# Eight batches of attention and MoE on one core: fixed attention tiles, a new order of steps, and joined tails

## The chip, the cores and the metric

The kernel runs on one core of a Trainium2 chip. The metric is the device time in microseconds. The program is one launch; nothing is computed on the host.

## What is computed

For each of 8 batches with 8 heads, 576 positions and a head width of 64, two attentions are added: one over q, k and v that are averaged in groups of four positions (144 positions, its result repeated four times), and a local one over the keys that lie at a distance under four. The sum, as a matrix x of 576 rows and 512 columns, goes through a mixing layer:

```python
s = scale * np.matmul(q, k.transpose(0, 1, 3, 2))
mask = np.abs(pos[:, None] - pos[None, :]) < factor      # local part
x = out_up + out_local                                   # (B, S, H * D)
theta = x @ w_theta
zr, zi = x * np.cos(theta), x * np.sin(theta)
y = np.einsum('ts,bsd->btd', w_tok_r, zr) + np.einsum('ts,bsd->btd', w_tok_i, zi)
u = x + y
return u + np.maximum(u @ w_ch, 0.0)
```

Inputs and output are float32; the kernel computes in bfloat16 with float32 sums.

## The kernel before

All eight batches run through one program that is pipelined over the batches by hand. Each kind of work is a Python generator, and a long string, `ORDER` (lines 80 to 88), says which generator takes its next step. After each step `pin` (line 695) chains every new instruction to the one before it on the same engine, so that every engine works in exactly the order of the string. The letters, with steps per batch:

- L (8) and v (5) load q, k and v; C (8) and w (5) cast them to bfloat16 on GpSimd (batch 0's q on ScalarE).
- A (4, `turns`, line 309) turns q and k so that the head width lies on the partitions: A.0 and A.2 are q, A.1 and A.3 are k. For most batches TensorE transposes nine blocks into PSUM; for the batches in `DMA_QK` a DMA transpose does it (q, `turn_qk`, line 284) into an SBUF tile of the staging pool. In both cases ScalarE copies the result in two halves into `qT` or `kT` (line 328), undoing a row order, and VectorE sums groups of four (line 336).
- B (1) averages v; Q (2) and N (3) are the scores and the result of the averaged attention; S (5, line 409) are the local scores: TensorE, then the exponential on ScalarE (line 432), then two selects on GpSimd that cut the band (lines 439 and 441; batch 0 has a mask from TensorE).
- V (5, `outputs`, line 487) is the local result: TensorE into PSUM, VectorE divides into `tmp` (line 508). `tmp` comes from a pool with four buffers; for the batches in `DMA_X` GpSimd first zeroes the rows that the division doesn't write (line 507).
- T (5, line 525) turns `tmp` and adds the averaged part into `xT` (line 542): TensorE and VectorE for most batches, a DMA transpose (t, line 293) and GpSimd for those in `DMA_X`.
- H (5, `phases`) is theta with cosine and sine on ScalarE (lines 564, 565; H.4 is the tail of 64 positions, with a DMA transpose, z). Z (4, `modulate`, line 592) turns x back, on TensorE (line 601) or, for the batches in `DMA_Z`, by one DMA transpose (x, line 301), and multiplies.
- X (5, `mix`, line 612) is the mixing over positions: X.0 to X.3 are 9 matmuls each over 512 columns (line 620), X.4 is 36 over the tail's 64 columns (line 626); VectorE adds x (lines 621, 628) into `uT`.
- u (2, line 631) turns `uT` by two DMA transposes, main part and tail. R (5, `channels`, line 643) multiplies by w_ch, R.4 for the tail with eight matmuls of 64 rows and 256 columns (line 658). O (5, `store`, line 665) adds on VectorE into `osb`, which has four buffers, and issues the stores; the tail has two.
- K, l, c, h, g, W are constants and weights: c.7 to c.11 are the casts of the second token weight on VectorE (line 241), W (9) its transposes. D (5) are warm-up matmuls.

All DMAs are issued by SyncE's queue, SP, in the order of the string. PSUM has two tiles of two banks (w2, taken in turn) and four of one bank (w1, taken in turn).

ScalarE's exponential and sine need different tables, so each change between S or Q and H loads one.

Of the kernel before, what the change touches and what calls it, by code (L numbers as in the profile page):

```python
# [10 lines left out]
BF16 = mybir.dt.bfloat16  # L11
AF = mybir.ActivationFunctionType
ALU = mybir.AluOpType
AX = mybir.AxisListType

P = 128
B = 8
H = 8
S = 576
D = 64  # L20
DM = 512
# [11 lines left out]
NCH = 5  # L33

WR = 9
# [6 lines left out]
HALF = 64  # L42
MAIN = 512
# [4 lines left out]
def kernel(  # L48
# [11 lines left out]
    nc = tc.nc  # L60

    const = ctx.enter_context(tc.tile_pool(name="const", bufs=1))
# [13 lines left out]
    def w1(name, dt=FP32):  # L76
# [1 line left out]


    ORDER = (  # L80
        "KLLLLCCLLKKKLCALCvCvvCCCDvvLLwLLAALLAlvlllSSLwLSwwwVBCCCCQQVNNlllAVcNvvvCTTAcvcTllCCSSHHVVDTTlllALHc"
        "chCccZLLLwwwAwwHHSSDZLzZDcBcSZDcWcLLLCvCCCcQVWWWvQWVCvvWCNWCCwSWWNVwwwXAAhXAvhNAhwLLXTSSLXQQTTLLBuVH"
        "VTggLCCLCgLLHvvgTCCCCCNNHHVHXSSRROzOZZZvLvLAwLLLLZARvvvvvACNSOXwwwASRuCCCSwVXVVOXQCCQCTSVTTTALABLSXA"
        "uTCvSRSwvHNNwHHCOVwwVZXwANLVCLHHRRLLLLQQLLCCCRROOOzOBVTLuSTCCLZLZSTSHNZNHVCXTTAAXvvvvLLAAHHCCwVCCCqw"
        "wLwHvwXzLLVZSXqZZLLCCCQqSuXvVNBROSQZTLTwXVVXNqvTvTTNAvLALASHHHVHwVuXvvHzXZCCwCCAwwSCSRNROXLqQSLqOZRC"
        "BCCqSOVTRTqQRvvuSSOOTZHZVVXTNTNAAHHXVVAHvwwwHtAtwXSSXXRRRRuuOOONOVtVzwTBZZSZRQQRVTSROROOOSSRttZNHNOu"
        "XTVTTNSRxOXHVVHHVtttZZHzXZZVXXXXTttTTuTTXHHRHxROOROuROZHZHRZzZOXXuXXXXuRuRROOOXRRRuOORRROOOORO"
    )

    staged = {}  # L90
# [98 lines left out]
    for i in range(2):  # L189
        t = const.tile([P, NCH, H, 66], BF16, name=f"v_w{i}")  # L190
        nc.vector.memset(t[:, :, :, 64:65], 1.0)
        v_ws.append(t)

    vds = []
    for i in range(2):
        t = const.tile([P, 2, H, 66], BF16, name=f"vd{i}")
# [82 lines left out]
    parts, turned = {}, {}  # L279


    DMA_QK, DMA_X, DMA_Z = (6, 7), (6, 7), (6, 7)

    def turn_qk(b):

# [23 lines left out]
    def turns(b):  # L309

        q_tm, k_tm = inputs.pop(b)
        qT = work.tile([P, 4, S], BF16, tag="qT", name=f"qT{b}")
        kT = kTs[b % 2]
        qdT = work.tile([P, 4, SD], BF16, tag="qdT", name=f"qdT{b}")
        kdP = kdPs[b % 2]
        parts[b] = (qT, kT, qdT, kdP)

        for j in range(4):
            n, i = j % 2, j // 2
            tm, To = ((q_tm, qT), (k_tm, kT))[n]  # L320
            if b in DMA_QK:
                ps = turned.pop((b, j)).rearrange("p r w -> p (r w)")
            else:
                ps = w2(f"pstr{n}{i}_{b}", BF16).rearrange("p k e -> p (k e)")[:, 0:WR * P]
                for r in range(WR):
                    nc.tensor.transpose(out=ps[:, P * r:P * r + P], in_=tm[:, i, r, :, :], identity=ident)  # L326
            for a in range(2):
                act(  # L328
                    out=To[:, 2 * i + a, 0:S].rearrange("p (w r) -> p w r", r=WR),
                    in_=ps.rearrange("p (r a w) -> p a w r", r=WR, a=2)[:, a],  # L330
                )
            hs = slice(2 * i, 2 * i + 2)
            dst, src = (qdT[:, hs, :], qT[:, hs, :]) if n == 0 else (kdP[:, hs, :, 0:30], kT[:, hs, :])
            src = src.rearrange("p e (m j) -> p e m j", j=4) if n == 0 else src.rearrange("p e (g m j) -> p e g m j", g=5, j=4)
            with nc.allow_low_precision(reason="sums are taken in float32 and rounded once"):
                nc.vector.tensor_reduce(out=dst, in_=src, axis=AX.X, op=ALU.add)  # L336
            yield
# [149 lines left out]
    def outputs(b):  # L487

        v_w = v_ws[b % 2]
        for c in range(NCH):  # L490
            kw, qn, cnt = KW[c], QN[c], QC[c]
            ps = w2(f"psloc{c}_{b}")
            pv = ps[:, :, 0:260].rearrange("p e (j w) -> p e j w", w=65)
            for h in range(H):
                blk, par = slot(h)
                nc.tensor.matmul(  # L496
                    out=pv[0:qn, h // 4, h % 4, :],
                    lhsT=pms[b][c][0:kw, 4 * par + blk, 0:qn],
                    rhs=v_w[0:kw, c, h, 0:65],
                    start=(h % 4 == 0), stop=(h % 4 == 3),  # L500
                )
            rl = work.tile([P, 2, 4], FP32, tag="rl", name=f"rl{c}_{b}")
            nc.vector.reciprocal(out=rl[0:cnt], in_=pv[0:cnt, :, :, 64])
            tmp = tmps[b, c] = work.tile([P, DM], BF16, tag="tmp", bufs=4, name=f"tmp{c}_{b}")
            if b in DMA_X:
                lo = 96 if c < 4 else 64
                nc.gpsimd.memset(tmp[lo:], 0.0)  # L507
            nc.vector.tensor_tensor(  # L508
                out=tmp[0:cnt].rearrange("p (e j d) -> p e j d", e=2, j=4),
                in0=pv[0:cnt, :, :, 0:D],  # L510
                in1=rl[0:cnt].unsqueeze(3).to_broadcast([cnt, 2, 4, D]),
                op=ALU.mult,
            )
            yield
        pms.pop(b)


    def parted(t):

        return (t[:, 0:4 * MAIN].rearrange("p (e t) -> p e t", e=4),  # L520
                t[:, 4 * MAIN:4 * S].rearrange("p (e t) -> p e t", e=4))
# [85 lines left out]
            yield  # L607


    uTs, urs = {}, {}  # L610

    def mix(b):

        (xA, xB), z = parted(xTs[b]), zs.pop(b)
        uT = uTs[b] = moep.tile([P, 4 * S], BF16, tag="uT", name=f"uT{b}")
        uA, uB = parted(uT)
        for dc in range(4):
            ps = w1(f"psu{dc}_{b}")
            for j in range(9):
                nc.tensor.matmul(out=ps, lhsT=z[:, j, P * dc:P * dc + P], rhs=WT[:, j, 0:MAIN], start=(j == 0), stop=(j == 8))  # L620
            nc.vector.tensor_tensor(out=uA[:, dc, :], in0=ps, in1=xA[:, dc, :], op=ALU.add)  # L621
            yield
        ps = w1(f"psut_{b}")[:, 0:4 * HALF].rearrange("p (e t) -> p e t", e=4)
        for dc in range(4):
            for j in range(9):
                nc.tensor.matmul(out=ps[:, dc, :], lhsT=z[:, j, P * dc:P * dc + P], rhs=WT[:, j, MAIN:S],  # L626
                                 start=(j == 0), stop=(j == 8))
        nc.vector.tensor_tensor(out=uB, in0=ps, in1=xB, op=ALU.add)
        yield

    def u_turn(b):

        ur = moep.tile([P, 16, P], BF16, tag="ur", name=f"ur{b}")
        utr = moep.tile([P, 2, P], BF16, tag="utr", name=f"utr{b}")
        urs[b] = ur, utr
        nc.sync.dma_start_transpose(out=ur, in_=uTs[b][:, 0:4 * MAIN])
        yield
        nc.sync.dma_start_transpose(out=utr, in_=uTs[b][:, 4 * MAIN:4 * S])
        yield

    rels = {}

    def channels(b):

        uA, uB = parted(uTs[b])
        for c in range(5):
            psr = rels[b, c] = w1(f"psr{c}_{b}")
            if c < 4:
                for dc in range(4):
                    nc.tensor.matmul(  # L650
                        out=psr, lhsT=uA[:, dc, P * c:P * c + P], rhs=wch[:, dc, :],
                        start=(dc == 0), stop=(dc == 3),
                    )
            else:

                for dc in range(4):
                    for hf in range(2):
                        nc.tensor.matmul(
                            out=psr[64 * hf:64 * hf + 64, 0:256], lhsT=uB[:, dc, :],
                            rhs=wch[:, dc, :].rearrange("p (j e d) -> p e j d", j=2, e=2)[:, hf],  # L660
                            start=(dc == 0), stop=(dc == 3),
                        )
            yield

    def store(b):

        ur, utr = urs.pop(b)
        for c in range(5):
            psr = rels.pop((b, c))
            osb = moep.tile([P, DM], FP32, tag="osb", bufs=4, name=f"osb{c}_{b}")  # L670
            n = 4 if c < 4 else 2
            nc.vector.scalar_tensor_tensor(  # L672
                out=osb[:, 0:P * n].rearrange("p (e d) -> p e d", d=P),
                in0=psr[:, 0:P * n].rearrange("p (e d) -> p e d", d=P), scalar=0.0,
                in1=ur[:, c:16:4, :] if c < 4 else utr, op0=ALU.max, op1=ALU.add,
            )
            if c < 4:
                nc.sync.dma_start(out=out[b, P * c:P * c + P, :], in_=osb)
            else:
                for hf in range(2):  # L680
                    nc.sync.dma_start(
                        out=out[b, 512:576, :].rearrange("t (j e d) -> e t j d", j=2, e=2)[hf],
                        in_=osb[64 * hf:64 * hf + 64, 0:2 * P].rearrange("p (j d) -> p j d", j=2),
                    )
            yield

    last = {}
# [57 lines left out]
```

## Time and profile before

| | us |
|---|---|
| median of 8 runs | 252.41 |
| lowest and highest | 250.55, 254.09 |
| the profiled execution's own time | 254.09 |
| its span in the profile | 252.4 |

The profile is of one execution. A row of the groups gives line, engine, operation, what is written and read with partitions x elements, then the busy time and the mean of one in ns, then the idle time just ahead of them and who ended it. A wait's row gives the total, the number of times and the longest. Matmuls overlap, so the busy time of TensorE (PE) is not its work at full speed. The granted TensorE clock is 0.985 in the mean.

### The profile page before, as it was taken

The page shows a single profiled execution, that of the slowest core. Times are in us where ns is not written, and L with a number is a line of the kernel's source. Part 1 is how long each engine was busy: PE and PEld are TensorE (multiplying, and loading weights), DVE is VectorE, ACT ScalarE, POOL GpSimd, SP SyncE. Part 2 cuts the span into 40 slices and gives each one's busy share as a digit, 9 for nine tenths or more (in the row PEclk, how much of TensorE's full clock was granted, in tenths as well). Part 3 has the DMA queues.
Part 4 walks back from the last instruction along what each step waited for, and adds up shares of the span by engine and source line. Part 5 has one row for each costly group of instructions (what it writes and reads, how often), then busy time and mean ns, then how long its engine had stood idle before and what let it go on. Part 6 is the DMA issues. An engine that isn't in the chain of part 4 may idle for free.

```text
span 252.4 us, 6628 instructions
## 1 busy us (share of the span) xinstructions
PE 225.8 (89%) x2602; PEld 136.1 (54%) x2602; DVE 185.5 (74%) x340; ACT 170.1 (67%) x250; POOL 166.9 (66%) x233
## 2 busy tenths in 40 slices
PE   0877799799999999999999999999769989999991
PEld 0535365466577566755657656565445645455450
DVE  3275788758979988898898898899676558365462
ACT  3595799438899559999688999899936781151000
POOL 4438764994898999899679666998199971600000
PEclk9999999779999999999999999999999999999999
DMA  6999989996496999899999999979691765965596
GB/s 209 291 298 359 289 236 350 240 236 229 42 293 171 321 157 246 187 298 223 297 235 271 210 204 225 262 108 216 128 270 35 229 96 101 137 202 117 65 269 198
DMA packets 100511, 53.94 MB, mean 214 GB/s; under 512 B 83968, under 2 KB 86016, under 8 KB 100480
## 3 DMA queue, kind: packets, MB, share of 16 engines
q1 hardware_dynamic: 100480, 53.53, 90.1%
q8 instruction: 20, 0.33, 0.6%
q14 instruction: 11, 0.09, 0.2%
HBM read 33.59 MB, written 9.44 MB: 170 GB/s over the span
## 4 chain that ended last, share of the span: by engine, by line
PE 60%; ACT 11%; DMA 9%; DVE 8%; POOL 8%; issue 2%; SPq 1%; DVEq 0%; POOLq 0%; ACTq 0%
PE psu L620 20%; PE psr L650 7%; PE psth L559 6%; PE pstr L326 4%; PE psloc L496 4%; DMA z<-zT 3%; PE psS L424 3%; ACT pm L432 3%; POOL pm L441 3%; POOL pm L439 2%; ACT qT L328 2%; PE psut L626 2%; DMA out_dram<-osb 2%; PE xTps L538 2%; DMA st_q<-in_q_dram 2%
## 5 line engine op out<-in xcount | busy, mean ns | idle before, releaser
L620 PE MATMUL psu<-WT,z 128*128 128x512 bf16 x288 | 66.8, 379 | 0.6 <-DMA z<-zT 0.6
L439 POOL TENSOR_SCALAR_AFFINE_SELECT pm<-pm 128x1024 bf16<-128x1024 bf16 (+1 forms) x35 | 36.7, 1048 | 21.7 <-ACT pm L432 21.7
L620 PEld LDWEIGHTS <-z 128*128 128x128 bf16 x288 | 26.5, 98 | 29.7 <-DMA z<-zT 1.1
L432 ACT ACTIVATE pm<-psS 128x1024 bf16<-128x1024 f32 (+1 forms) x40 | 37.9, 980 | 5.4 <-PE psS L424 5.0
L441 POOL TENSOR_SCALAR_AFFINE_SELECT pm<-pm 128x1024 bf16<-128x1024 bf16 (+1 forms) x35 | 36.6, 1046 | 2.4
L508 DVE TENSOR_TENSOR tmp<-psloc,rl 120x512 bf16<-120x512 f32 (+2 forms) x40 | 27.6, 690 | 7.6 <-POOL tmp L507 6.0
L650 PE MATMUL psr<-wch,uT 128*128 128x512 bf16 x128 | 30.8, 380 | 1.4 <-DVE uT L621 1.4
L564 ACT ACTIVATE cs<-psth,pihc 128x512 bf16<-128x512 f32 x32 | 22.3, 697 | 14.1 <-PE psth L559 11.4
L559 PE MATMUL psth<-wth,xT 128*128 128x512 bf16 x128 | 31.6, 379 | 0.0
L621 DVE TENSOR_TENSOR uT<-psu,xT 128x512 bf16<-128x512 f32 x32 | 21.8, 685 | 12.7 <-PE psu L620 12.6
L336 DVE TENSOR_REDUCE qdT<-qT 128x288 bf16<-128x1152 bf16 x16 | 21.5, 1346 | 10.1 <-ACT qT L328 10.1
L131 POOL CAST v_w<-st_v 128x512 bf16<-128x512 f32 (+1 forms) x40 | 23.9, 621 | 4.5 <-DMA st_v<-in_v_dram 4.3
L124 POOL CAST k_tm<-st_k 128x576 bf16<-128x576 f32 x32 | 21.5, 671 | 7.4 <-DMA st_k<-in_k_dram 6.0
L672 DVE SCALAR_TENSOR_TENSOR osb<-psr,ur 128x512 f32<-128x512 f32 x32 | 21.4, 685 | 6.2 <-PE psr L650 4.8
L336 DVE TENSOR_REDUCE kdP<-kT 128x300 bf16<-128x1200 bf16 x16 | 22.3, 1395 | 4.7 <-ACT kT L328 4.7
L328 ACT COPY qT<-pstr 128x576 bf16<-128x576 bf16 x24 | 14.2, 648 | 11.8 <-PE pstr L326 11.7
L124 POOL CAST q_tm<-st_q 128x576 bf16<-128x576 f32 x28 | 18.8, 672 | 3.4 <-PE pstr L326 2.1
L565 ACT ACTIVATE cs<-psth 128x512 bf16<-128x512 f32 x32 | 19.4, 606 | 0.0
L650 PEld LDWEIGHTS <-uT 128*128 128x128 bf16 x128 | 11.5, 98 | 14.0 <-issue 1.9
L496 PEld LDWEIGHTS <-pm 128*128 128x128 bf16 (+1 forms) x320 | 14.6, 104 | 8.2 <-DVE tmp L508 1.6
L496 PE MATMUL psloc<-v_w,pm 128*128 128x65 bf16 (+1 forms) x320 | 16.5, 198 | 2.4 <-DVE tmp L508 1.1
L542 DVE TENSOR_TENSOR xT<-xTps,xdT 128x480 bf16<-128x480 bf16 (+3 forms) x36 | 18.2, 547 | 0.5 <-PE xTps L538 0.4
(92 smaller groups left out, 399.2 us busy)
## 6 DMA issues: line engine op xcount, KB each, us to landing
st_q<-in_q_dram SPq DMA_DIRECT2D x32, 288.0 KB, 5.4
st_k<-in_k_dram SPq DMA_DIRECT2D x32, 288.0 KB, 5.6
st_v<-in_v_dram SPq DMA_DIRECT2D x32, 256.0 KB, 5.8
out_dram<-osb SPq DMA_DIRECT2D x32, 256.0 KB, 2.7
st_v<-in_v_dram SPq DMA_DIRECT2D x8, 192.0 KB, 5.0
tok<-in_moe_w_tok_r_dram SPq DMA_DIRECT2D x4, 288.0 KB, 8.4
tok<-in_moe_w_tok_i_dram SPq DMA_DIRECT2D x4, 288.0 KB, 4.2
th<-in_moe_w_theta_dram SPq DMA_DIRECT2D x2, 512.0 KB, 7.6
```

What stands on the lines that cost most here:

```text
L124: eng[i](out=dst[:, hh // 2, :, hh % 2, :], in_=staged.pop((b, f"{'qk'[i]}{hh}")).rearrange("p (r d) -> p r d", d=D))
L131: gp(out=v_ws[b % 2][0:KW[c], c, :, 0:D], in_=staged.pop((b, f"v{c}"))[0:KW[c], 0:DM].rearrange("p (h d) -> p h d", d=D))
L336: nc.vector.tensor_reduce(out=dst, in_=src, axis=AX.X, op=ALU.add)
L432: nc.scalar.activation(out=pv, in_=ps[0:kw].rearrange("p e (j w) -> p (e j) w", w=P)[:, :, 0:qn], func=AF.Exp, scale=SCL,)
L439: nc.gpsimd.affine_select(out=pv, in_=pv, compare_op=ALU.is_ge, fill=0.0, base=off, pattern=[[0, 8], [-1, qn]], channel_multiplier=1)
L441: nc.gpsimd.affine_select(out=pv, in_=pv, compare_op=ALU.is_ge, fill=0.0, base=6 - off, pattern=[[0, 8], [1, qn]], channel_multiplier=-1)
L496: nc.tensor.matmul(out=pv[0:qn, h // 4, h % 4, :], lhsT=pms[b][c][0:kw, 4 * par + blk, 0:qn], rhs=v_w[0:kw, c, h, 0:65], start=(h % 4 == 0 ...
L508: nc.vector.tensor_tensor(out=tmp[0:cnt].rearrange("p (e j d) -> p e j d", e=2, j=4), in0=pv[0:cnt, :, :, 0:D], in1=rl[0:cnt].unsqueeze(3) ...
L559: nc.tensor.matmul(out=th, lhsT=xA[:, dc, P * c:P * c + P], rhs=wth[:, dc, :], start=(dc == 0), stop=(dc == 3),)
L564: nc.scalar.activation(out=cs[:, 0, :], in_=th, func=AF.Sin, bias=pihc, scale=1.0)
L620: nc.tensor.matmul(out=ps, lhsT=z[:, j, P * dc:P * dc + P], rhs=WT[:, j, 0:MAIN], start=(j == 0), stop=(j == 8))
L650: nc.tensor.matmul(out=psr, lhsT=uA[:, dc, P * c:P * c + P], rhs=wch[:, dc, :], start=(dc == 0), stop=(dc == 3),)
```

## The change

Besides the new order string, with 683 letters for 694:

- `tmp` is one of five fixed tiles, one for each chunk, whose unwritten rows are zeroed once at the start on VectorE; the memsets in the loop go.
- For the batches in `DMA_QK` (6 and 7) ScalarE copies q with the loops exchanged, and VectorE copies k.
- Batch 5 joins `DMA_Z`.
- The tail of u is kept in a tile of two batches; the turn, the channel product, the add and the two stores of the tails are done once for each pair, after the odd batch.
- In the order string, among others: batch 0's k turn A0.1 stands before the first warm-up step, c8 to c11 stand before Z0.3, S7.0 to S7.4 stand earlier among X4, R3 and R4, and x6.0 stands before three of batch 4's stores, t7 and z6.0.

```diff
-    DMA_QK, DMA_X, DMA_Z = (6, 7), (6, 7), (6, 7)
+    DMA_QK, DMA_X, DMA_Z = (6,7),(6,7),(5,6,7)
...
+    tmp5 = []
+    for c in range(NCH):
+        t = const.tile([P, DM], BF16, name=f"tmp{c}")
+        nc.vector.memset(t[96 if c < 4 else 64:], 0.0)
+        tmp5.append(t)
...
-                act(
-                    out=To[:, 2 * i + a, 0:S].rearrange("p (w r) -> p w r", r=WR),
-                    in_=ps.rearrange("p (r a w) -> p a w r", r=WR, a=2)[:, a],
-                )
+                dst = To[:, 2 * i + a, 0:S].rearrange("p (w r) -> p w r", r=WR)
+                src = ps.rearrange("p (r a w) -> p a w r", r=WR, a=2)[:, a]
+                if b not in DMA_QK:
+                    act(out=dst, in_=src)
+                elif n == 0:
+                    act(out=dst.rearrange("p w r -> p r w"), in_=src.rearrange("p w r -> p r w"))
+                else:
+                    dve(out=dst, in_=src)
...
-            tmp = tmps[b, c] = work.tile([P, DM], BF16, tag="tmp", bufs=4, name=f"tmp{c}_{b}")
-            if b in DMA_X:
-                lo = 96 if c < 4 else 64
-                nc.gpsimd.memset(tmp[lo:], 0.0)
+            tmp = tmps[b, c] = tmp5[c]
...
+        if b % 2 == 0:
+            uBs[b // 2] = moep.tile([P, 4, 2, HALF], BF16, tag="uB", name=f"uB{b // 2}")
+        uB = uBs[b // 2][:, :, b % 2, :]
...
-        nc.sync.dma_start_transpose(out=utr, in_=uTs[b][:, 4 * MAIN:4 * S])
+        if b % 2:
+            utr = utrs[b // 2] = moep.tile([P, 4, P], BF16, tag="utr", name=f"utr{b // 2}")
+            nc.sync.dma_start_transpose(out=utr, in_=uBs[b // 2].rearrange("p e i t -> p (e i t)"))
...
-        for c in range(5):
+        for c in range(4 + b % 2):
             psr = rels[b, c] = w1(f"psr{c}_{b}")
...
+            for dc in range(4):
+                nc.tensor.matmul(
+                    out=psr, lhsT=uA[:, dc, P * c:P * c + P] if c < 4 else uBs[b // 2][:, dc],
+                    rhs=wch[:, dc, :], start=(dc == 0), stop=(dc == 3),
+                )
...
+                for i in range(2):
+                    nc.sync.dma_start(out=out[b - 1 + i, 512:576, :], in_=osb[HALF * i:HALF * i + HALF])
```

More of the change, by code (lines that the diff above doesn't have):

```diff
@@ L80 @@
     ORDER = (
[L81 to L87, printed above, removed]
+        "KKLLLLCCCCLAALLLvCCvvKCKDwvvLLLCLLLLAALSwwwSwlVVCBClllQQCCvNNllllAANvvvvTSllTSCCccSVHVVCCDlTTcclAccL"
+        "LcTwZwwwwALhHHHcLLLLHSQZZDDQBSDzvLCChWcCCccCCgCScWCNWWSWWvvvwvVWNLWWZwwwwVvALLXAAXVhAhXSSXVNBQTTTggS"
+        "TQHVVHLLLCTCHuLgCCCCCNNLCLLHvvZVHSwXROZzROvvAAZZARALwLLLRCCLwLvvSwwvCvCOSLLOXCCCCSSXVVXAABQNXQVTTSTw"
+        "SuwTTSHVHNNZZLALXAHVNHvwCVHRwQvvuCwwwLLLzLRQRCCOCBSOOZSZTTTARvCCLALwSLHHCvOVXVvLTNLvvLLXTNAHHZZVwwCA"
+        "CCwqXHCCCvvVSXZzZQSXVLLNTBqQCLLqwVTTCLROqAuSSTCvHHVNXTwNCCCLLVAAHHqAHXSSXXXZSZVLqwwvvRRONVSRQzvvOOZS"
+        "TTLQBCCCVqCROTqSZHVVTuXTNwVAwwwHHHxANAAHvSROXXSSwXzQSRRuuOVOZNQXSSBZZZtttRRTOOVVXTRRVRSRttTOTTxONNHO"
+        "OXHVVHHVVttHZZZNZzXXXtttTuXXXTTTHTxHHROROHuRROOZHzZZZROXXXXXXuuRRROOOXuRRRROROOOROO"
     )
@@ L607, in modulate @@
             yield
-    uTs, urs = {}, {}
+    uTs, uBs, urs, utrs = {}, {}, {}, {}
     def mix(b):
         (xA, xB), z = parted(xTs[b]), zs.pop(b)
-        uT = uTs[b] = moep.tile([P, 4 * S], BF16, tag="uT", name=f"uT{b}")
-        uA, uB = parted(uT)
+        uT = uTs[b] = moep.tile([P, 4 * MAIN], BF16, tag="uT", name=f"uT{b}")
+        uA = uT.rearrange("p (e t) -> p e t", e=4)
+        if b % 2 == 0:
+            uBs[b // 2] = moep.tile([P, 4, 2, HALF], BF16, tag="uB", name=f"uB{b // 2}")
+        uB = uBs[b // 2][:, :, b % 2, :]
         for dc in range(4):
@@ L631, in u_turn @@
     def u_turn(b):
[L633 to L636, printed above, removed]
+        ur = urs[b] = moep.tile([P, 16, P], BF16, tag="ur", name=f"ur{b}")
+        nc.sync.dma_start_transpose(out=ur, in_=uTs[b])
         yield
-        nc.sync.dma_start_transpose(out=utr, in_=uTs[b][:, 4 * MAIN:4 * S])
-        yield
+        if b % 2:
+            utr = utrs[b // 2] = moep.tile([P, 4, P], BF16, tag="utr", name=f"utr{b // 2}")
+            nc.sync.dma_start_transpose(out=utr, in_=uBs[b // 2].rearrange("p e i t -> p (e i t)"))
+            yield
@@ L641 @@
     rels = {}
     def channels(b):
-        uA, uB = parted(uTs[b])
-        for c in range(5):
+        uA = uTs[b].rearrange("p (e t) -> p e t", e=4)
+        for c in range(4 + b % 2):
             psr = rels[b, c] = w1(f"psr{c}_{b}")
[L648 to L662, printed above, removed]
+            for dc in range(4):
[3 more added lines that the diff above has]
+                )
@@ L663, in channels @@
             yield
     def store(b):
-        ur, utr = urs.pop(b)
-        for c in range(5):
+        ur = urs.pop(b)
+        for c in range(4 + b % 2):
             psr = rels.pop((b, c))
             osb = moep.tile([P, DM], FP32, tag="osb", bufs=4, name=f"osb{c}_{b}")
-            n = 4 if c < 4 else 2
             nc.vector.scalar_tensor_tensor(
-                out=osb[:, 0:P * n].rearrange("p (e d) -> p e d", d=P),
-                in0=psr[:, 0:P * n].rearrange("p (e d) -> p e d", d=P), scalar=0.0,
-                in1=ur[:, c:16:4, :] if c < 4 else utr, op0=ALU.max, op1=ALU.add,
+                out=osb.rearrange("p (e d) -> p e d", d=P),
+                in0=psr.rearrange("p (e d) -> p e d", d=P), scalar=0.0,
+                in1=ur[:, c:16:4, :] if c < 4 else utrs.pop(b // 2), op0=ALU.max, op1=ALU.add,
@@ L679, in store @@
             else:
[L680 to L684, printed above, removed]
+                for i in range(2):
+                    nc.sync.dma_start(out=out[b - 1 + i, 512:576, :], in_=osb[HALF * i:HALF * i + HALF])
             yield
```

## The prediction

> Steps are named by their letter in ORDER, batch and number: X4.0 is the first chunk of batch 4's mix, A7.3 the last turn of batch 7's k.
>
> **What bounds the kernel now.** I read the page first, and of it the slices.
>
> ```profile
> span 252.4 us, 6628 instructions
> PE 225.8 (89%) x2602; PEld 136.1 (54%) x2602; DVE 185.5 (74%) x340; ACT 170.1 (67%) x250; POOL 166.9 (66%) x233
> PE   0877799799999999999999999999769989999991
> ```
>
> PE is busy nearly all the time, with three holes: the start, slices 28 to 30 (177 to 195 us), and the end. Then I cut the span at four PE steps whose start the timeline gives: X0.0 (54.45), X4.0 (164.74), X6.0 (212.99) and R7.4 (246.33), and asked for busy time by stage.
>
> ```profile
> 0.00:54.45 54.45, 40.52 (x462) 25.22 (x463) 33.52 (x80) 36.94 (x57) 35.35 (x62) 0.94 1.01 280
> 54.45:164.74 110.29, 107.75 (x1407) 68.63 (x1403) 96.90 (x162) 92.98 (x138) 91.17 (x123) 1.00 1.01 227
> 164.74:212.99 48.25, 43.55 (x496) 25.38 (x495) 35.74 (x69) 34.99 (x46) 35.54 (x45) 1.00 0.72 151
> 212.99:246.33 33.34, 33.34 (x246) 16.48 (x242) 17.68 (x30) 5.22 (x10) 4.81 (x6) 1.00 0.72 155
> 246.33:252.40 6.07, 0.63 (x9) 0.36 (x8) 1.70 (x3) 0.00 (x0) 0.00 (x0) 0.93 0.64 205
> ```
>
> Columns: length, then busy time of PE, its loads, DVE, ACT, POOL. Busy PE hides short waits, so I priced each PE step by its spacing where it runs undisturbed: in the PE timeline 36 psu matmuls go from 229.85 to 237.62 (X: 1.94 per chunk), 12 psr ones from 237.62 to 240.21 (R: 0.86), the mix's tail takes 1.05, a channel tail 0.56, a Z 0.22. Added up over all steps this is 211.5 us of PE work: 33.2 before X0.0, 102.7 to X4.0, 42.0 to X6.0, 33.0 to R7.4. So PE loses 7.3 + 14.0 us before X0.0, 7.6 to X4.0, 6.3 to X6.0 and 0.3 after: the last 39 us are PE alone. Who causes these losses is in the waits (us in total, times, longest):
>
> ```profile
> POOL pm L439 <- ACT pm L432: 21.7, 9, 5.9
> DVE tmp L508 <- POOL tmp L507: 6.0, 4, 2.1
> PE psvb L347 <- POOL v_w L131: 2.2, 1, 2.2
> PE wps L258 <- DVE wtm L241: 1.8, 2, 1.0
> PE psr L650 <- DVE uT L621: 1.4, 1, 1.4
> ```
>
> The longest one lies at 175.95 to 181.89: POOL stands still for ACT's exponentials of S6.3, because ACT is then copying batch 7's turned q and k. After that POOL has no gap until 207 and PE follows it.
>
> ```profile
> L328 ACT COPY kT<-pstr 128x576 bf16<-128x576 bf16 x24 | 14.4, 661 | 2.1 <-PE pstr L326 2.1
> L328 ACT COPY kT<-qk 128x576 bf16<-128x576 bf16 x8 | 9.3, 1237 | 0.0
> L328 ACT COPY qT<-qk 128x576 bf16<-128x576 bf16 x8 | 9.3, 1210 | 0.0
> L658 PE MATMUL psr<-wch,uT 128*64 128x256 bf16 x64 | 5.0, 279 | 0.0
> L507 POOL MEMSET tmp<- 32x512 bf16 x8 | 3.9, 519 | 0.2
> L564 ACT ACT_TABLE_LOAD x8 | 10.3, 1283 | 2.0 <-issue 1.9
> ```
>
> By shape: a copy from the DMA-turned tile (qk, in SBUF, read at a stride of 128 elements) costs 1.2 us, from PSUM 0.66.
>
> [...] two in 0.82 us before POOL's selects begin at 41.27, then two in 2.48 us beside them.
>
> ```profile
> 40.53 0.82 DVE L241 CAST wtm<-tok 128x576 bf16<-128x576 f32 x2
> 42.63 2.48 DVE L241 CAST wtm<-tok 128x576 bf16<-128x576 f32 x2
> ```
>
> [...] The trace shows 0.50 from 47 to 53 us, just after PE waited for the casts.
>
> **The change, part by part.**
> PE work. Eight channel tails go (8 x 0.56 = 4.5), four full chunks come (4 x 0.86 = 3.5), batch 5's four Z transposes go (0.9): 211.5 becomes 209.5. By stage, in the built order: 33.4, 102.1, 40.4, 32.8.
>
> ACT. The eight k copies leave (9.3 us); two table loads go, 14 for 16 (2.6 us). The q copies read along the row and write at a stride of 9 elements: between 0.66 (the PSUM row) and 1.21 (as now); I take 0.75, 3.7 us less. ACT had no gap over 0.7 us from 131 to 182, so here this counts.
>
> POOL. Ten memsets, 4.9 us, go. Seven stood between 185 and 207, where POOL is the chain: 3.6 us on the path. Five zeroings on DVE come at the start, beside the 5.5 us in which DVE waits for the first copy (each about 0.27, as warm's): nothing; without that cover 1.4.
>
> DVE. Four tails for eight, 0.6 less. Eight k copies come, an unseen form. Low bound 0.45 (the DVE copy of WT, L263, same size, from PSUM); high bound 1.35 (a cast beside POOL). I take 0.85, 6.8 us in all: the low bound times the stride penalty that ACT shows (1237 / 661). They are not hidden by idle DVE (4 us idle in 143 to 184); what covers them is the order: A6.1 to A6.3 stand while PE has H4.2 to X3.4 (about 11 us in other PSUM banks), A7.0 to A7.3 while it has H5.1 to X4.3 (10 us). Behind them wait H4.4, X3.1, O3.0 and X4.1, and PE for their banks. Without the cover the 6.8 us would be on the path.
>
> SP and DMA. Four tail transposes and eight stores fewer, one turn of batch 5's x more (4.7 us to land, like the two now). x5.0 holds SP for 3 us before v7.4 and O3.0; v7.4 then lands about 17 us after X4.0 starts, and POOL reaches it at 18: nothing, but up to 2 us on POOL's chain without that margin. An even batch's tail waits for the odd batch's; the last pair is 6 and 7, whose mixes end the kernel anyway: nothing beyond R7.4's 0.3. V7.0 to V7.4 now wait for t6.0 to t6.4 to land, each on its own tile; O4.0 and N7 are queued behind V7.0 on DVE. The t6 stand in SP ahead of O4.0, and by the built order PE has 13 us of work between V6.4 and V7.4: nothing, else 2.5 (the landing in the table of issues). x6.0 now stands before O4.1 to O4.3, t7.0, t7.1 and z6.0: all wait for T6.4. The four osb buffers cover the stores; z6.0 is on X6.0's path (below).
>
> Stages. To X0.0: the casts c8 to c11 no longer wait for Z0.3 (its 0.69 and the 0.67 before it), and A0.1 stands ahead of the warm-up. c11 landed at 40.91, c11's cast ended at 46.4: POOL's selects still meet the casts. I take 2.0 of 14.0 off, bounds 0 and 4: 54.45 - 2.0 + 0.2 (work) = 52.7.
> X0.0 to X4.0: work -0.6; losses 7.6 to 7.0, since ACT is freed and DVE loaded: 1.2 less, bounds -2.5 and 4.
> X4.0 to X6.0, counted from X4.0: with A7.1 and A7.3 gone ACT reaches S6.3 at about 11 to 13 (now 16), POOL then has 21 us to T6.4 (S6.3 to S7.4 14.4, w7.4 0.6, B7.0 1.2, five T6 4.9) and ends at 33 to 34, PE needs it at 34. x6.0 (3 us of SP), three stores (1.4), t7.0, t7.1 (2.4), z6.0 (1.2 and 2.4 to land) end at 43 to 44.5, PE needs them at 42. Losses 2.1 for 6.3, and 1.6 less work: 5.8 less, bounds 2 and 7.5. After the stall is gone POOL, DVE and PE are late together.
> X6.0 to the end: work -0.25, stalls -0.2; the last store no longer queues behind a ninth osb tile: R7.4 to the end 5.7 for 6.07. 0.8 less.
> Sum: 1.8 + 1.2 + 5.8 + 0.8 = 9.6 of the span's 252.4. The profiled run took 254.09, 1.7 more than its span; the median of eight is 252.41. Taken from the median: 242.8.
>
> **Rivals.**
> A, DVE as the bound (chance 0.18): the copies cost 1.35, since POOL is busy for 18.3 of the 20 us from 155 to 175. 8 x 0.5 = 4 us come back: 246.8. Against it: DVE work from X0.0 to X5.2 would be about 140 us where PE has 138.
> B, the waits move (0.11): a new order brings its own losses, and only the PE work and the end remain: 252.4 - 1.9 - 0.6 = 249.9. For it: PE's losses are a fraction of a us at many places. Against: two of the larger, 2.2 and 1.4, have a cause that is removed.
> C, slower (0.07),[...] 0.85 x 1.34 / 0.45 = 2.5 us a copy[...]. 8 x (2.5 - 0.85) = 13.2: 256.0. It decides from 2.2 us a copy on. Against: waiting for one POOL instruction adds about 0.9, not a factor.
> That the change doesn't do what it says: the built order has the 14 loads, no memset on POOL and 36 stores' adds, so no.
>
> **How the numbers follow.** The forecast, 0.64, is 242.8, by itself 240 to 247. The range leaves out C, half of B and a tenth below: 239.0 to 250.0. A measurement tells about 0.5% (1.3 us) from no change: faster 0.88 (forecast, A, most of B), same 0.05, slower 0.07.
>
> **What would show it.** Right: the POOL gap before S6.3 under 3 us, X0.0 near 52.7, X4.0 to X6.0 near 42.5, DVE copies L328 near 0.85, PE losses near 20. Wrong: copies over 1.3, PE waiting for uT or osb of batches 3 and 4 (A), or X6.0 waiting over 2 us for z by way of x6.0.

## The result, and the profile after

The kernel after takes 256.14 us in the median of 11 runs (255.01 to 259.2), the kernel before 252.9 in runs on the same chips. The ratio is 1.0133, 95% interval 1.0104 to 1.0161: slower, by 3.4 us (1.3%). The forecast was 242.8.

First the head and the slices of the page of after, in the columns that the prediction explains, with the granted clock of TensorE as a third row.

```profile
span 254.7 us, 6457 instructions
PE 226.0 (89%) x2538; PEld 133.7 (52%) x2538; DVE 190.7 (75%) x349; ACT 169.7 (67%) x240; POOL 162.4 (64%) x223
PE   0777999999999999999995999998299999999990
PEclk9999999999999999999997799999779999999998
```

The hole of before (slices 28 to 30) is still there, in slice 28 now, deeper; another has come in slice 21. Around each of the two the clock falls. Now the stages, cut at the same four PE steps (X0.0, X4.0, X6.0, R7.4); the last three columns are the granted clock, the DMA share and GB/s.

```profile
0.00:49.29 49.29, 36.83 (x464) 23.47 (x464) 33.18 (x84) 36.76 (x57) 32.10 (x57) 1.00 1.04 280
49.29:164.69 115.40, 111.29 (x1394) 69.34 (x1392) 99.86 (x169) 94.53 (x134) 97.25 (x129) 0.97 1.03 233
164.69:214.55 49.86, 43.97 (x457) 24.39 (x454) 38.58 (x68) 33.19 (x40) 28.17 (x33) 0.93 0.68 142
214.55:247.59 33.04, 32.94 (x234) 16.21 (x231) 16.44 (x28) 5.22 (x10) 4.85 (x6) 1.00 0.71 154
247.59:254.70 7.11, 1.02 (x4) 0.29 (x3) 2.59 (x4) 0.00 (x0) 0.00 (x0) 0.86 0.67 221
```

To X0.0 the kernel after is 5.2 us ahead (54.45 before). It gives 5.1 back by X4.0 (115.40 for 110.29), 1.6 more by X6.0 (49.86 for 48.25) and 1.0 at the end (7.11 for 6.07). So the main losses lie between X0.0 and X6.0, where the prediction put 7.0 of its 9.6 us of gain. The waits of after say who causes them (us in total, times, longest):

```profile
POOL pm L449 <- ACT pm L442: 27.7, 7, 11.4
DVE qdT L346 <- ACT qT L339: 8.7, 3, 3.5
PE psS L434 <- ACT pm L442: 4.7, 1, 4.7
PE psloc L506 <- ACT pm L442: 3.5, 3, 2.8
DVE osb L671 <- DMA out_dram<-osb: 2.6, 2, 2.1
```

POOL's wait for ScalarE's exponentials, 21.7 before, should have shrunk; it has grown, and its longest from 5.9 to 11.4. The two PE rows are new. All of them name ScalarE. Its copies, by shape:

```profile
L339 ACT COPY qT<-qk 128x576 bf16<-128x576 bf16 x8 | 21.4, 2939 | 0.0
L341 DVE COPY kT<-qk 128x576 bf16<-128x576 bf16 x8 | 4.9, 650 | 0.0
L197 DVE MEMSET tmp<- 32x256 uint32 x4 | 1.1, 272 | 0.1
```

The q copy with exchanged loops takes 2.9 us, where it took 1.2 with the old loops (L328 before, 1210 ns). Eight of them keep ScalarE busy for 21.4 us instead of 9.3. The k copy on VectorE, on which the prediction spent most of its doubt, takes 0.65, and a zeroing of a fixed tile 0.27. ScalarE's part of the timeline around the longest wait (start, length, instruction):

```profile
166.48 5.35 ACT L339 COPY qT<-qk 128x576 bf16<-128x576 bf16 x2
...
174.72 5.31 ACT L339 COPY qT<-qk 128x576 bf16<-128x576 bf16 x2
...
180.52 1.28 ACT L442 ACT_TABLE_LOAD   x1
181.81 2.80 ACT L442 ACTIVATE pm<-psS 128x1024 bf16<-128x1024 f32 x3
182.91 1.09 POOL L449 TENSOR_SCALAR_AFFINE_SELECT pm<-pm 128x1024 bf16<-128x1024 bf16 x1 [11.41 <-ACT pm L442]
```

A7.0 and A7.2, the two q turns of batch 7, hold ScalarE for 5.3 us each. The maps of S6.3 stand behind them, POOL has nothing to cut until 182.91, and TensorE, which needs ScalarE to empty the score banks, stops as well:

```profile
137.07 0.77 PE L506 MATMUL psloc<-v_w,pm 96*92 96x65 bf16 x8 [2.77 <-ACT pm L442]
...
182.89 0.61 PE L434 MATMUL psS<-qT,kT 64*128 64x128 bf16 x8 [4.70 <-ACT pm L442]
183.43 4.02 PE L630 MATMUL psu<-WT,z 128*128 128x512 bf16 x9
```

The first of these stops, of 2.77 us, stands in the same way behind the q turns of batch 6. The last row is X4.3: nine matmuls that take 1.94 elsewhere take 4.02 after the stop; X3.0 after the first stop takes 4.04. That is the halved clock, of which the prediction saw one stretch in before: the granted clock is 0.50 for 6.8 us each, from 136.7 and from 181.0, so each of the two stops is paid for once more, with about 2 us. The clock fell 2.4 us into the first stop and 2.8 us into the second.

### The profile page after: what moved, and what is told of

The parts are those of the page before. It is cut to its first block, busy times and chain, and to the rows that moved or that the text cites. A ratio compares the mean times of both kernels' runs of the same rounds, so it can differ in the third digit from the quotient of the medians.

```text
span 254.7 us, 6457 instructions
## 1 busy us (share of the span) xinstructions
PE 226.0 (89%) x2538; PEld 133.7 (52%) x2538; DVE 190.7 (75%) x349; ACT 169.7 (67%) x240; POOL 162.4 (64%) x223
## 4 chain that ended last, share of the span: by engine, by line
PE 66%; ACT 17%; DVE 9%; DMA 3%; issue 3%; SPq 1%; DVEq 0%; ACTq 0%
PE psu L630 21%; PE psth L566 9%; PE psr L659 9%; PE psloc L506 4%; PE psS L434 4%; PE pstr L332 3%; ACT qT L337 3%; ACT kT L337 3%; PE psut L636 3%; ACT pm L442 3%; PE xTps L545 2%; DMA st_q<-in_q_dram 2%; ACT qT L339 2%; PE psnd L468 2%; PE wps L264 1%
## 5 line engine op out<-in xcount | busy, mean ns | idle before, releaser
L630 PE MATMUL psu<-WT,z 128*128 128x512 bf16 x288 | 70.0, 395 | 0.0
L630 PEld LDWEIGHTS <-z 128*128 128x128 bf16 x288 | 27.8, 101 | 32.3 <-issue 4.4
L346 DVE TENSOR_REDUCE qdT<-qT 128x288 bf16<-128x1152 bf16 x16 | 21.6, 1351 | 19.1 <-ACT qT L337 10.4
L571 ACT ACTIVATE cs<-psth,pihc 128x512 bf16<-128x512 f32 x32 | 22.8, 713 | 12.1 <-PE psth L566 10.4
L339 ACT COPY qT<-qk 128x576 bf16<-128x576 bf16 x8 | 21.4, 2939 | 0.0
L434 PE MATMUL psS<-qT,kT 64*128 64x128 bf16 (+1 forms) x320 | 15.3, 219 | 5.3 <-ACT pm L442 4.7
## 6 DMA issues: line engine op xcount, KB each, us to landing
st_v<-in_v_dram SPq DMA_DIRECT2D x32, 256.0 KB, 6.2
out_dram<-osb SPq DMA_DIRECT2D x32, 256.0 KB, 3.3
```

Of the source, the lines that this page charges most:

```text
L339: act(out=dst.rearrange("p w r -> p r w"), in_=src.rearrange("p w r -> p r w"))
```

## The experiments

Theory after the traces: the exchanged loops of the q copy are the whole of the slowdown, and the rest of the change would have been faster. Rivals: the copy is slow because it stands beside other work, not by its form; VectorE would have become the bound anyway; the tails or the new order cost what is lost.

To compare stages over kernels I use VectorE's add after X0.0, X4.0 and X6.0 (2.1 to 2.2 us after the PE steps' start) and the PE start of R7.4. "Forecast" is the prediction's own sum in that form.

| | to X0.0 | to X4.0 | to X6.0 | to R7.4 | to the end | span |
|---|---|---|---|---|---|---|
| before | 56.7 | 110.2 | 48.3 | 31.2 | 6.1 | 252.4 |
| forecast | 54.9 | 109.1 | 42.5 | 30.7 | 5.7 | 242.8 |
| after | 52.0 | 114.9 | 49.9 | 30.9 | 7.1 | 254.7 |
| q in the old loops | 52.2 | 110.2 | 43.5 | 30.8 | 7.1 | 243.8 |
| q and k as before | 52.7 | 111.7 | 48.7 | 31.0 | 7.4 | 251.4 |
| before, k on VectorE | 55.7 | 112.7 | 46.7 | 31.2 | 6.0 | 252.3 |
| before, joined tails | 54.3 | 110.7 | 49.1 | 30.6 | 7.3 | 252.0 |

### Only the q loops undone

```diff
-                    act(out=dst.rearrange("p w r -> p r w"), in_=src.rearrange("p w r -> p r w"))
+                    act(out=dst, in_=src)
```

> The changed kernel with one line undone: ScalarE copies batch 6's and 7's turned q with the loops of before (read at a stride of 128 elements, written in a row). Theory (the exchanged loops are the cause): the eight copies go from 2.7 us of ScalarE each to 1.2, about 11.7 us in all; the waits for ScalarE ahead of X3.0 and X4.3 and the two stretches at half clock behind them go; X0.0 to X4.0 falls from 115.4 to about 110, X4.0 to X6.0 from 49.9 to about 44; in all 243 to 247 us. Rival (the new order or the copies on VectorE are the cause): 253 us or more.

Measured: 245.43 us (244.85 to 245.58), ratio 0.9755 (0.973 to 0.9779). Here are the slices of its page, then its two copies, then POOL's wait.

```profile
span 243.8 us, 6424 instructions
PE   0866899999999999999999998999898999999990
PEclk9999999999999999999999999999999999999996
```

```profile
L339 ACT COPY qT<-qk 128x576 bf16<-128x576 bf16 x8 | 9.3, 1220 | 0.0
L341 DVE COPY kT<-qk 128x576 bf16<-128x576 bf16 x8 | 5.7, 750 | 0.0
```

```profile
POOL pm L449 <- ACT pm L442: 13.4, 8, 5.8
```

One line of the change is worth 10.7 us (256.14 to 245.43; 9.5 by the two ratios). ScalarE's copies differ by 21.4 - 9.3 = 12.1 us of busy time. Records of neighbours overlap, so the spacing tells more: from the start of a copy to the start of ScalarE's next instruction it is 2.2 to 2.6 us in the kernel after and 1.1 with the old loops, 10.4 us over the eight. So about all of that was on the path. The two holes and the halved clock behind them are gone. The rest of the change gains 2.4%.

### Only the q loops done

```diff
+                if b in DMA_QK and n == 0:
+                    act(out=dst.rearrange("p w r -> p r w"), in_=src.rearrange("p w r -> p r w"))
+                else:
+                    act(out=dst, in_=src)
```

> The kernel before with nothing but the exchanged loops in ScalarE's q copies. Theory: ScalarE has no idle time from 131 to 182 us there, so most of 8 x 1.46 = 11.7 us lands on the path: 258 to 265 us. Rival (the exchange matters little, the order does): 251 to 255 us.

Measured: 264.16 us, ratio 1.0532 (1.0463 to 1.0601), as expected. The row of its groups:

```profile
L331 ACT COPY qT<-qk 128x576 bf16<-128x576 bf16 x8 | 21.4, 2936 | 0.0
```

Same duration in another order of work, so the form costs it, wherever it stands. The loss is larger (13 us), perhaps because ScalarE still has its k copies here; no run separates that.

### The copies by themselves

> The copies alone: all of the computation is left out, and VectorE, then ScalarE, then GpSimd copy 128 x 576 bfloat16 from SBUF to SBUF, four times in each form: a row to a row; read at a stride of 128 elements as before (turn_read); written at a stride of 9 as in the change (turn_write); and written with every 2nd, 4th, 9th and 16th element. Theory: on ScalarE turn_write takes about 2.7 us, turn_read 1.2, a row 0.67; if single 2-byte writes are what costs, step2 is as slow as step9; if it is the distance, the time grows from step2 to step16. On VectorE turn_read takes 0.65. Rival (the 2.7 us came from contention with the other engines in the kernel): ScalarE's turn_write takes 0.7 to 1.3 here.

This kernel leaves the whole computation out: it only copies 128x576 bf16 from SBUF to SBUF, each engine in turn while the others stand, four times per form. `turn_read` is the old loops (read at a stride of 128 elements, write along the row), `turn_write` the exchanged ones (read along the row, write at a stride of 9), `row_row` has no stride.

```profile
L79 POOL COPY pool_turn_write<-after_act 128x576 bf16<-128x576 bf16 x4 | 10.8, 2707 | 0.0
L79 ACT COPY act_turn_write<-after_dve 128x576 bf16<-128x576 bf16 x4 | 10.8, 2700 | 0.0
L79 DVE COPY dve_turn_write<-src 128x576 bf16<-128x576 bf16 x4 | 6.2, 1544 | 0.0
L76 ACT COPY act_turn_read<-after_dve 128x576 bf16<-128x576 bf16 x4 | 4.6, 1155 | 0.0
L76 POOL COPY pool_turn_read<-after_act 128x576 bf16<-128x576 bf16 x4 | 4.6, 1141 | 0.0
L82 ACT COPY act_row_row<-after_dve 128x576 bf16<-128x576 bf16 x4 | 2.7, 668 | 4.6 <-DVE after_dve L84 4.6
L76 DVE COPY dve_turn_read<-src 128x576 bf16<-128x576 bf16 x4 | 2.5, 632 | 0.0
L82 DVE COPY dve_row_row<-src 128x576 bf16<-128x576 bf16 x4 | 1.2, 301 | 0.0
```

The 2.7 us are there with every other engine idle: no clash with other work, but the form of the write. (In the kernel after, the first copy of each pair takes 2.76 to 2.80 us and only the second, behind the first, 3.08 to 3.14.) It is worse than the strided read by a factor of 2.3 on ScalarE and of 2.4 on VectorE.

A last set of copies reads along the row and writes at a chosen step. Their single records depend on the copy ahead: directly behind one that writes at a step of 9, whose record is still open for about 0.5 us, a record is 0.3 us longer (at a step of 4, 1757 for 1456 ns; at 16, 2887 for 2595). Apart from those, ScalarE took 1456 ns at a step of 4 elements, 2765 at 9 and 2595 at 16 (668 at 1). The copies at a step of 2 took 1122, but all of them stand directly behind a `turn_write`, so some 0.3 us of that, by estimate from the two differences, is not theirs.

So on ScalarE a step of 4 elements already costs 1456 ns for 668, one of 9 costs 2765, and from 9 to 16 (2595) the cost grows no more. Why it stops there, the runs don't show; what a step of 2 costs by itself they don't settle.

### Both copies on VectorE

```diff
-                    act(out=dst.rearrange("p w r -> p r w"), in_=src.rearrange("p w r -> p r w"))
+                    dve(out=dst, in_=src)
```

> The changed kernel with batch 6's and 7's q copied by VectorE as well, with the loops of before. Theory: ScalarE is rid of 21.4 us, VectorE gets 8 x 0.65 = 5.2 us: 243 to 248 us; against the kernel with the loops alone undone it tells whether VectorE or ScalarE is the tighter of the two now. Rival (VectorE is the bound, or its copies hold up GpSimd): 252 us or more.

Measured: 254.3 us, ratio 1.0109 (1.008 to 1.0139). The expectation was missed: VectorE is the tighter engine. Its copies, and the new wait:

```profile
L339 DVE COPY qT<-qk 128x576 bf16<-128x576 bf16 x8 | 8.1, 1054 | 0.0
L341 DVE COPY kT<-qk 128x576 bf16<-128x576 bf16 x8 | 6.0, 790 | 0.0
```

```profile
PE psS L434 <- DVE kT L341: 3.7, 2, 2.8
```

Eight more microseconds on VectorE cost 8.9 of time against the old q loops on ScalarE. TensorE stops for k, and its granted clock is 0.963 in the mean of the profiled execution, for 0.992 with the old q loops on ScalarE. The copies are also longer here than the 0.65 expected: the longest two, of 2.43 and 1.55 us, begin while POOL is at work (more on that below). So the prediction's rival A (VectorE as the bound, by copies beside POOL) is real; it needs twice the copies.

### Both copies as before, the rest new

```diff
-                    act(out=dst.rearrange("p w r -> p r w"), in_=src.rearrange("p w r -> p r w"))
+                    act(out=dst, in_=src)
...
-                    dve(out=dst, in_=src)
+                    act(out=dst, in_=src)
```

> The changed kernel with both q and k of batches 6 and 7 copied by ScalarE with the loops of before. Theory: with the loops alone undone VectorE has no idle time from X3.0 to X5.1 and is the bound there; without the k copies it is freed of 5.7 us, but ScalarE gets 9.8 us and holds up S6.3 again: 246 to 250 us. Rival (it makes no difference which of the two copies k): 244.5 to 246 us.

Measured: 253.24 us, ratio 1.005 (1.0017 to 1.0083), slower than I expected and than before. Its wait of POOL:

```profile
POOL pm L449 <- ACT pm L442: 23.1, 8, 8.3
```

Without k's move the rest of the change gains nothing. In the table 5.2 of the 7.6 us to the run with k on VectorE lie between X4.0 and X6.0 (48.7 for 43.5): there ScalarE's copies stand ahead of S6.3, as the prediction said.

### Only k's move, in the old order

```diff
-                act(
+                (dve if b in DMA_QK and n == 1 else act)(
```

> The kernel before, with only the k copies of batches 6 and 7 moved from ScalarE to VectorE (their loops, the tiles, the order and the tails as before). Theory: this move is the part of the change that earns, with q left in the old loops: ScalarE gives up 9.8 us, VectorE takes about 8 x 0.75 = 6 us; the maps of S6.3 come sooner and the time falls to 247 to 250. Rival: VectorE has no room in the old order of the steps, and what ScalarE gains is lost there: 251.5 or more.

Measured: 253.36 us, ratio 1.0022 (0.9993 to 1.0051): the rival was right. Copies and wait:

```profile
L328 DVE COPY kT<-qk 128x576 bf16<-128x576 bf16 x8 | 8.0, 1040 | 0.0
```

```profile
POOL pm L439 <- ACT pm L432: 17.3, 8, 4.7
```

The stage of S6.3 gains 1.6 us and the stage before it loses 2.5. So the move and the rest of the change need each other: the move alone gives nothing, the rest alone costs 0.5% (though it holds the fixed tiles, which alone gain, as the next run shows), together they gain 2.4%. Which part of the rest makes the room, the order above all, was not tried apart.

The copies also cost more here, 1.04 us for 0.75, and the kept traces show with what. In the eight profiles that have such copies on VectorE, all 39 that began while POOL had no instruction under way took 0.63 to 0.67 us. Of the 27 that began beside one under way, 23 took 0.79 to 2.43. In this run four of the eight copies were such long ones. Here are two of its copies, and POOL's select:

```profile
179.59 2.12 DVE L328 COPY kT<-qk 128x576 bf16<-128x576 bf16 x2
180.10 1.10 POOL L439 TENSOR_SCALAR_AFFINE_SELECT pm<-pm 128x1024 bf16<-128x1024 bf16 x1 [2.60 <-ACT pm L432]
```

The first copy began ahead of the select and took 0.65; the second began 0.05 us behind it and took 1.56. That is 0.91 us more beside one POOL instruction, the about 0.9 that the prediction named against its rival C.

### Only the fixed tiles

```diff
...
-            tmp = tmps[b, c] = work.tile([P, DM], BF16, tag="tmp", bufs=4, name=f"tmp{c}_{b}")
-            if b in DMA_X:
-                lo = 96 if c < 4 else 64
-                nc.gpsimd.memset(tmp[lo:], 0.0)
+            tmp = tmps[b, c] = tmp5[c]
```

> The kernel before with nothing but the five fixed tiles in place of the memsets in the loop. Theory of the prediction: seven memsets, 3.6 us, leave GpSimd's chain between 185 and 207: 249 to 251 us. Rival (GpSimd's memsets lie in its idle time or another wait takes their place): 251.5 to 253 us.

Measured: 249.14 us, ratio 0.9887 (0.9847 to 0.9927): 2.9 us of gain, interval 1.8 to 3.9, as expected.

### Only the joined tails

The tails of two batches in one tile, one turn, one product and one add, as in the change; from the old order string only the letters that fall away are taken out.

```diff
...
-        for c in range(5):
+        for c in range(4 + b % 2):
...
```

> The kernel before with the joined tails alone; the order string is that of before without the letters of the even batches' tails. Theory: 1.0 us of TensorE work less, 0.3 of it after X6.0, and one osb tile less in the last stores: 0.5 to 1.5 us less than before. Rival (the stores at the end land no earlier, and TensorE has its losses elsewhere): no change, within 0.5 us.

Measured: 253.51 us, ratio 1.0043 (1.0009 to 1.0077): missed, it costs 1.1 us (interval 0.2 to 1.9). From R7.4 to the end it takes 7.3 us where before takes 6.1, and that is the end of every kernel with joined tails in the table. The last stretch of after shows what stands there, first SP, then VectorE:

```profile
240.29 1.82 SPq L644 DMA_TRANSPOSE ur<-uT  x1
242.21 2.02 SPq L677 DMA_DIRECT2D out_dram<-osb  x3
244.32 2.01 SPq L648 DMA_TRANSPOSE utr<-uB  x1
246.45 3.89 SPq L677 DMA_DIRECT2D out_dram<-osb  x5
250.79 1.14 SPq L680 DMA_DIRECT2D out_dram<-osb  x2
```

```profile
246.85 1.96 DVE L671 SCALAR_TENSOR_TENSOR osb<-psr,ur 128x512 f32<-128x512 f32 x3 [2.08 <-DMA out_dram<-osb]
```

Batch 6's stores stand on SP behind the turn of batch 7's u (1.8 us, 1.3 before), and O6.3's behind the joined tail's turn too (2.0 us, 1.3 before); three of them land after 4.0 to 4.5 us (2.9 to 3.5 before). O7.0 waits 2.1 us for a buffer of theirs, the adds trail the matmuls, and the last add is of 512 columns (0.69 us) where it was of 256 (0.42).

### Six buffers for the stores

```diff
-            osb = moep.tile([P, DM], FP32, tag="osb", bufs=4, name=f"osb{c}_{b}")
+            osb = moep.tile([P, DM], FP32, tag="osb", bufs=6, name=f"osb{c}_{b}")
```

This one and those below have the q copies in the old loops.

> The changed kernel with the loops undone and six osb buffers in place of four. In the run with the loops undone VectorE waited 1.96 us for a buffer before O7.0, and R7.4 to the end took 7.05 us where the prediction had 5.7. Theory: the wait goes, and 1 to 1.5 us with it: 244 to 244.5 us. Rival (the stores themselves, behind two turns of u, are what ends late): no change from 245.4, within 0.4 us.

Measured: 245.59 us, ratio 0.9736 (0.9686 to 0.9786), the same as with four buffers (245.43), as the rival had it. VectorE and SP at its end:

```profile
238.88 0.69 DVE L671 SCALAR_TENSOR_TENSOR osb<-psr,utr 128x512 f32<-128x512 f32 x1 [0.41 <-DMA utr<-uB]
```

```profile
236.73 2.75 SPq L677 DMA_DIRECT2D out_dram<-osb  x5
239.60 1.31 SPq L680 DMA_DIRECT2D out_dram<-osb  x2
```

The wait for a buffer ahead of O7.0 is gone (a later one of 0.4 us remains), and the last add now waits for the turned tail instead. The seven stores go out within some 4 us, and the last five land after 3.1 to 3.75 us where they took 2.1 to 2.7 with four buffers. End of the kernel 6.8 us for 7.1: the transfers are late in place of the buffers.

### Batch 5's x on TensorE again

The letter of its step x5.0 leaves the order string too.

```diff
-    DMA_QK, DMA_X, DMA_Z = (6,7),(6,7),(5,6,7)
+    DMA_QK, DMA_X, DMA_Z = (6,7),(6,7),(6,7)
```

> The kernel after with the q copies in the old loops (245.4), and batch 5's x transposed on TensorE again rather than by the DMA transpose. Theory: TensorE does 0.9 us more, and ScalarE or VectorE the copies out of PSUM: 0.5 to 1.5 us above 245.4. Rival: the cover is there, no difference that can be told (within 0.5 us).

Measured: 246.3 us (246.19 to 246.62), ratio 0.977 (0.9721 to 0.9818). The medians differ by 0.9 as expected, but the intervals of the ratios overlap: not settled.

### Two k copies elsewhere

```diff
-                    dve(out=dst, in_=src)
+                    (gp if (b, j) == (7, 3) else dve)(out=dst, in_=src)
```

> The kernel after with the q copies in the old loops (245.4), and the last two k copies of batch 7 on GpSimd instead of VectorE. Theory: VectorE sets the time in the stages of batches 4 to 6 of this kernel, and it gives up 2 x 0.75 us, while GpSimd, which waits there for ScalarE, takes 2 x 1.14 us: 243.5 to 245. Rival: the copies hold up GpSimd's sums in the maps, or VectorE is not what sets the time: 245.4 or more.

Measured: 245.58 us (244.14 to 246.54), ratio 0.9752 (0.9687 to 0.9816): no difference that can be told, though its profiled span (242.4) is the shortest of all. Its copies and POOL's wait:

```profile
L341 POOL COPY kT<-qk 128x576 bf16<-128x576 bf16 x2 | 2.7, 1368 | 0.0
```

```profile
POOL pm L449 <- ACT pm L442: 9.5, 6, 2.4
```

POOL's longest wait falls from 5.8 to 2.4 us, and from X4.0 to X6.0 nothing changes (43.4 for 43.5): that wait no longer sets the time there. The second version also takes A6.3's k copies to ScalarE.

```diff
-                    dve(out=dst, in_=src)
+                    (gp if (b, j) == (7, 3) else act if (b, j) == (6, 3) else dve)(out=dst, in_=src)
```

> As the run with the last k copies of batch 7 on GpSimd, and the last two k copies of batch 6 on ScalarE (2 x 1.2 us). Theory: VectorE gives up 3 us in all: 242.5 to 244.5. Rival: ScalarE is held up ahead of the maps of S6.3 by 2.4 us and the gain is lost: 245.5 or more.

Measured: 246.49 us (245.99 to 247.04), ratio 0.9776 (0.9724 to 0.9827): nothing gained, as the rival had it.

## Why the prediction was wrong

The runs with the exchanged loops alone undone and alone done, and the copies by themselves, show the cause. By stage, after against the forecast: -2.9 to X0.0, +5.8 to X4.0, +7.4 to X6.0, +0.2 to R7.4, +1.4 at the end; together 11.9 us of span. With the q loops undone they are -2.7, +1.1, +1.0, +0.1 and +1.4: 1.0 us in all. That flatters the rest of the prediction, for the gains were read in an execution of before that took 254.09, 1.7 above the median from which they were then taken off. In time the kernel with the loops undone takes 245.43, 2.6 above the forecast, and by the ratio the rest of the change gains 6.2 of the 9.6 us that were forecast for the whole.

- **The step that failed**: "between 0.66 (the PSUM row) and 1.21 (as now); I take 0.75". The copy takes 2.4 us from its start to the next instruction's (2.9 by its record): far above the upper bound. It was to free 3.7 us of ScalarE; it held it for 10.4 more, and the runs with that line alone undone and alone done show 9.5 to 13 us of time for it. The lower bound came from a row that has its stride on the read side, in PSUM; the upper one took for granted that a new form can't be worse than the old. No row of before showed a strided write to SBUF of this kind, so there was no ground for an upper bound of "as now". The effect was one-sided too: two stops of TensorE cost a halved clock on top (0.50 for 6.8 us each).
- **ScalarE, the rest**: k's copies gone (9.3 us) and 14 table loads, as predicted. That this counts ahead of S6.3 is right, by the runs with and without it: 5.2 us there.
- **VectorE**: 0.85 was taken for k's copies, by way of a stride penalty; 0.65 to 0.82 came in the new order, 0.65 where POOL was not at work and more only beside it. The 0.65 of the kernel after is luck: POOL stood still, waiting for ScalarE, whenever one of its eight copies began. The zeroings took 0.27, as predicted. The idle time of VectorE from 143 to 184 was 5 us (41.0 less 36.0 busy), not 4. The cover by the order was just enough: with q there too the time rises by 8.9 us.
- **POOL**: 3.6 us on the path were predicted from the memsets; the tiles alone give 2.9 (1.8 to 3.9).
- **To X0.0**: 2.0 us of losses were taken off; the kernel after is 5.2 ahead by the PE step. About half of that, by estimate, is the half clock from 47 to 53 us, which the profile of before has and that of after has not (clock 0.94 and 1.00 in that stage): the run of before with joined tails has nearly the old order up to there and shows no half clock in that stretch (its 32 full matmuls of the W steps, most of which lie there, take 220 ns in the mean, for 279 in before; with a mean clock of 0.984 it has some elsewhere), and reaches X0.0 after 54.3 on the table's scale, the kernels with the new order and q or k as before after 52.2 to 52.7. The order's own part is thus near the 2.0; the price of a halved clock was left out of the sum.
- **The tails and stores**: "nothing beyond R7.4's 0.3", and a gain of 0.35 at the end. Wrong: the tails alone cost 1.1 us. The last store no longer queues behind a ninth buffer, but the O7 adds queue behind batch 6's stores, and the last piece is twice as long. Six buffers alone gained nothing: the transfers were then late instead.
- **SP and x5.0**: "nothing": the run that takes x5 back is 0.9 higher, not told apart from none.
- **Rivals**: C's number (256.0) is met by coincidence, not by its cause: it had 2.5 us for a copy on VectorE, and those took 0.65. A's engine did become the next limit, as the run with both copies there shows. B's number (249.9) is not met, and with the q loops undone the time stands below it. Of its mechanism the end of the kernel shows a part: there the wait moved to the stores.
- **The range**: it held neither the time nor this cause. With an upper bound of 3 us for an unseen form on ScalarE (eight times 2.25 us above what was taken) it would have reached to 261.

## What to carry to other kernels

When loops of a copy are exchanged, the stride goes from the read to the write side, and that was not free here (2.9 us for 1.2 on ScalarE): price the new form by a row of the same engine with the same stride on the same side, or keep its upper bound open. On an engine that has no idle time ahead of what others wait for, one such line can eat the gain of the whole change, and the stops of TensorE behind it (2.8 and 4.7 us) were paid for once more here, by a halved clock (about 2 us each). Parts of a change can need each other (a move and the order that makes room for it), so undo one part of the new kernel as well as do it alone in the old one.

## What the runs showed of the hardware that I had not expected

- A bf16 copy in SBUF that writes at a stride of 9 elements takes 2700 ns on ScalarE, 2707 on GpSimd and 1544 on VectorE; reading at a stride of 128 elements takes 1155, 1141 and 632, no stride 668, 667 and 301. ScalarE and GpSimd run alike in all three.
- Already a step of 4 elements on the write side costs ScalarE 1456 ns for 668, and 1757 directly behind a copy that writes at a step of 9: a slow write also lengthens the record of the copy behind it, by 0.3 us.
- The same copy form on VectorE took 0.65 to 0.82 us in the new order of work and 1.04 in the old one, 0.63 with all others idle. The long ones go with GpSimd: no copy that began with GpSimd free took over 0.67 us, and 23 of the 27 that began beside a running GpSimd instruction took 0.79 or more.
- The last seven stores (five of 256 KB, two of 128) took 2.1 to 2.8 us each to land with four buffers, and 2.7 to 3.75 with six, when all went out within some 4 us.
- The half clock (0.50) inside the kernels before and after came in stretches of 6.8 us, one and two of them. In before two waits of TensorE, of 0.8 and 1.0 us and 0.2 apart, stand just ahead of it (from 46.7). They don't always bring it: the run with joined tails has two such waits for the same casts (1.8 us in all), and its W matmuls take 220 ns for 279.
